# Moving steps on the time line of a hand-ordered attention and Fourier-mixing kernel

## The chip, the core and the metric

The kernel runs on one core of one Trainium2 chip. A core has five engines that each work through their own list of instructions in order: TensorE (PE in the profile: matmuls and transposes, with PEld for its weight loads), VectorE (DVE), ScalarE (ACT), GpSimd (POOL) and SyncE (SP), which here only issues DMA transfers. An instruction that needs what another engine makes waits for a semaphore, and everything behind it on its engine waits with it. The metric is the device time of one execution in microseconds (us), the median of several runs.

## The reference

Two parts follow each other. The first is an attention without a square score matrix, the second mixes tokens and columns with a Fourier transform and ends in a two-layer network:

```python
# q, k, v: (8 batches, 8 heads, 576 tokens, 64)
q_s = softmax(q, axis=-1)
k_s = softmax(k, axis=tokens)
kv  = einsum('bhsd,bhse->bhde', k_s, v)
att = einsum('bhsd,bhde->bhse', q_s, kv)
x   = att as (8, 576, 512)

u   = x + real(fft(fft(x, axis=1), axis=2))
un  = (u - mean(u)) / sqrt(var(u) + 1e-6)        # over the 512 columns
out = u + relu(un @ w_ch1) @ w_ch2               # 512 -> 2048 -> 512
```

All of it is float32.

## The kernel before

**Tiles.** A batch's 576 tokens are 512 in four tiles of 128, and 64 left over. The left-over tokens of two batches share a tile ("shared tokens"); the eight such halves make a ninth group of 512 tokens. So the network runs over nine groups of 512 tokens in the order 0 to 6, the shared group, 7. Group 0 is worked as plain matmuls while the weights arrive. The eight that follow are called stages 1 to 8 here. Stage n works the network of its group, and beside it the attention, Fourier mixing and normalization of the next one (in the code b = order + 1), so stage 2 prepares batch 3, stage 3 batch 4, and so on. Stage 7 has only the norm of the last group beside it, stage 8 nothing.

**A stage.** The two layers are an *up* half (`up`) and a *down* half (`down`). Both use Strassen's scheme in Winograd's form: seven products of quarter matrices in the order 1, 6, 5, 7, 2, 4, 3 in place of eight, with sums before and after. Their products collect in three PSUM banks: products 1 and 2 in `ba`, 6, 7 and 4 in `bb`, 5 and 3 in `bc`. Product 7 adds onto what 6 left in its bank, so an engine has to have read the sum of 6 (u2 = bb + s1, L1137 in the up half, L1290 in the down half) before 7 may begin, and the same holds for 4 after 7 (u3). The final sums of the up half are L1178 on DVE, and ACT's ReLU (L1179, L1174) follows; POOL forms the input sums of the next layer (`a_side`, L389 to L392). The down half of stages 2 to 7 (`deep_down`) applies the scheme twice: one plain product (`single`, L1262), then six of the inner problems in three units of two, each with seven products (L1283). Before a unit its inputs need four sums per product (`a_step`, L1238), three on DVE and one on POOL. After a unit POOL adds results into x (`into`, L1242). Stage 1 cuts the second layer's weights for this on the way (`deepen`, L1202) and writes them to device memory (L1208, w2d), from where later stages read them (L447).

**Work beside the products.** For each next batch: four key blocks (`k_load` L577 to L591, `k_exp` L618 to L630, `k_turn`, `k_times_v`), four query tiles (`q_load` L694, `q_exp` L719 to L738, `q_turn`, `q_times_kv`), and for even batches the shared tokens' tile (`t_load`, `t_turn` L766, `t_fold` L778 to L787, then `t_times_kv` L823 to L838). Then `folded` adds and subtracts mirrored tokens and columns (L854, L860, L869, L875, L876), `block` multiplies by the token table (L910, L913), `mix_own` and `mix_shared` by the column table (L947, L950, with the copy L956, the sums L968/L969 and the additions into x L980/L981). Last comes `norm`: statistics (L1001, L1002), root (L1005), scales (L1008, L1009), a dummy exponential that brings ACT's exponential table back (L1016), normalized tile (L1030), transposes on PE (L1036), their copies (L1044), and four sums for Strassen's scheme (`combine`, L396 to L399), which the next stage's up half reads.

**What sets the order.** From stage 1 on there is no scheduler: `timed` gives every step a number, its time on a script, all steps are sorted by it, and each engine gets its instructions in that order. A number is a place in a list, not a time of the hardware: an instruction runs when its engine reaches it and its data is there. An up half is 56 units long (`UP`), a deep down half 50 (`TWICE`), and two units hold one up product. The steps' own lists (`return [(0, top), (0.8, exp), (4.5, inverse)]`) are relative, and `at(t, ...)` moves them. The attention of the next batch has a `start` and an `end` of 45 within the stage: 0 in stage 1, -7 (in the stage ahead) in the later ones. All loads and most stores are issued from the SP list, so a load can also stand behind a store that waits. A stored tile whose tokens run backwards goes through device memory: written to a `mirror` tensor (L1418), then read back reversed (L1420), which must wait until the first transfer has landed.

Of the kernel before, what the change touches and what calls it, by code (L numbers as in the profile page):

```python
# [93 lines left out]
def at(t, script):  # L94
    return [(t + dt, step) for dt, step in script]
# [42 lines left out]
class _Block:  # L138
# [356 lines left out]
    def attention_timed(self, b, start, end):  # L495

        keys = [("k", b, r) for r in range(NR)]
        tail = [("t", b)] if b % 2 == 0 else []
        own = [("q", b, c, u) for c in range(2) for u in range(2)]
        first = start + 14 + 5 * len(tail)  # L500
        gap, steps = (end - 13 - first) / 3, []
        for i, it in enumerate(keys):
            t = start + 3.5 * i
            steps += at(t - 5.5, self.k_load(it)) + at(t, self.k_exp(it)) + at(t + 4, self.k_turn(it))
            steps += at(t + 7, self.k_times_v(it))
        for it in tail:
            t = start + 14
            steps += at(t - 6.5, self.t_load(it)) + at(t, self.q_exp(it)) + at(t + 8, self.t_turn(it))
            steps += at(t + 10, self.t_fold(it))
        for i, it in enumerate(own):  # L510
            t = first + gap * i
            steps += at(t - 6.5, self.q_load(it)) + at(t, self.q_exp(it)) + at(t + 8, self.q_turn(it))
            steps += at(t + 11, self.q_times_kv(it))
        return steps + at(start + 14 + (23 if tail else 15), self.t_times_kv(b))

    def second_keys(self):

# [326 lines left out]
    def folded(self, b):  # L844


        nc, V, G = self.nc, self.nc.vector, self.nc.gpsimd
        eo = self.eo.setdefault(b, {})

        def tokens_folded(some):  # L850
            for i in some:
                e, op = ((V if b == 0 else G), ALU.add) if i < 2 else (V, ALU.subtract)
                eo[i] = self.halves()
                e.tensor_tensor(out=eo[i][:, 0:D], in0=self.xpart(b, i % 2, 0), in1=self.xpart(b, i % 2, 1), op=op)  # L854

        def columns_folded(some):
            for i in some:
                e, op = ((V if b == 0 else G), ALU.add) if i < 2 else (V, ALU.subtract)
                t = eo[i]
                e.tensor_tensor(out=t[:, 1:HD], in0=t[:, 1:HD], in1=t[:, D - 1:HD:-1], op=op)  # L860
                if b == 0 and i > 1:
                    self.warm(t[:, 0:HD], 2)

        def by_frequency(some):

            for i in some:
                e, op = ((G, ALU.add), (G, ALU.subtract), (V, ALU.add), (V, ALU.subtract))[i]
                one, two = eo[i // 2 * 2], eo[i // 2 * 2 + 1]
                (V if b == 0 else e).tensor_tensor(out=eo[i][:, NN:], in0=one[:, 0:NN], in1=two[:, 0:NN], op=op)  # L869

        def columns_again(some):

            for i in some:
                t, y = eo[i], eo[i][:, NN:]
                V.tensor_tensor(out=t[:, 0:QD], in0=y[:, 0:QD], in1=y[:, HD:QD:-1], op=ALU.subtract)  # L875
                V.tensor_tensor(out=y[:, 0:QD], in0=y[:, 0:QD], in1=y[:, HD:QD:-1], op=ALU.add)  # L876

        def fetch():
            if b == 0:
                self.folded_at = eo[1][:, NN:]  # L880
            elif b + 1 < B:
                self.keys_from(b + 1, eo[1])

        steps = []
        for some, times in ((2, 3), (1, 4.5, 6, 8)), ((0, 1), (0, 4, 6, 12)):
            for f, t in zip((tokens_folded, columns_folded, by_frequency, columns_again), times):
                steps.append((t, lambda f=f, some=some: f(some)))
        return steps + [(12.2, fetch)]
# [103 lines left out]
    def norm(self, g):  # L992
# [4 lines left out]
        uns, box = {}, {}  # L997
# [67 lines left out]
            put(9, scales, s)  # L1065
            put(9.1, back)
        for n, i in enumerate((0, 2, 1, 3)):
            put(10 + 2 * n, normal, i)
            put(12 + 2 * n, turn, i)
            put(12.8 + 2 * n, laid, i)  # L1070
        put(20, combine)
        return steps

    def norm_steps(self, g):
# [139 lines left out]
    def deep_down(self, g, order):  # L1214
# [100 lines left out]
        for i, unit in enumerate(UNITS):  # L1315
            t = 8 + n * i
            for k, o in enumerate((4, 5, 2, 6)):
                for j, m in enumerate(unit):
                    put((0 if i == 0 else t - n + 2) + 3 * k + j * 1.2 + 0.3, a_step, m, o)
            for k, o in enumerate(ORDER):  # L1320
                for j in range(2):
                    put(t + 2 * k + j, product, unit, o, j)
                put(t + 2 * k + 1.5, ends, unit, o)
        t = 8 + n
        put(t + 1, into, 1, 0, 4)
        put(t + 3, into, 0, 0, 2)
        t += n
        put(t + 1, sums, 6, 1)
        put(t + 3, into, 0, 1, 6)
# [69 lines left out]
    def store(self, g, c, u, x, d=None):  # L1399
# [17 lines left out]
            box.append(t[:, s])  # L1417
            e.dma_start(box[0], x())  # L1418

        return [(0, there), (5, lambda: e.dma_start(cols(out)[:, ::-1, :], cols(box[0])))]  # L1420


@with_exitstack
def kernel(ctx: ExitStack, tc: tile.TileContext, q, kT, v, w1, w2, ft,
# [24 lines left out]
    def timed(t, order, g):  # L1449
# [2 lines left out]
        if order == B:  # L1452
            return steps + [(t + 6 + 1.2 * i, lambda i=i: blk.later and blk.later.pop(0)()) for i in range(36)]
        if b == B:
            return steps + at(t + UP + 24, blk.norm(groups[b]))
        start, end = -7 if order > 1 else 0, 45
        steps += at(t, blk.attention_timed(b, start, end)) + at(t + end, blk.folded(b))
        t += UP
        for i, k in enumerate((2, 3, 0, 1, 4)):
# [2 lines left out]
        if b % 2:  # L1462
            mixes.insert(0 if b == B - 1 else 2, blk.mix_shared(b // 2))
        for i, some in enumerate(mixes):
            steps += at(t + 13 + 4 * i, some)
        return steps + at(t + 24, blk.norm(groups[b]))

    fetch, convert = blk.weights()

# [127 lines left out]
```

## Time and profile before

The time before is 1136.15 us, the median of three runs (1134.88 to 1137.81). The profiled execution spans 1130.9 us.

| half | from, us | length, us |
|---|---|---|
| stage 1 up, down | 194.5, 256.9 | 62.4, 59.1 |
| stage 2 up, down | 316.0, 387.9 | 72.0, 57.5 |
| stage 3 up, down | 445.4, 512.1 | 66.7, 56.1 |
| stage 4 up, down | 568.2, 631.0 | 62.8, 57.5 |
| stage 5 up, down | 688.5, 756.7 | 68.2, 56.1 |
| stage 6 up, down | 812.8, 875.6 | 62.8, 57.6 |
| stage 7 up, down | 933.2, 981.6 | 48.4, 47.4 |
| stage 8 up, down | 1029.0, 1077.4 | 48.4, 50.0 |

A half is counted from its first product (L1167 for up; L1361, L1262 or L1283 for down) to the first of the next. In the profile, matmuls are pipelined and each fp32 matmul leaves two records, so a busy share says less than the distance between the starts of neighbours: a longer distance than usual is a hole. A line of the timeline has start and length in us, the engine, the line of the code, the operation, written tile <- read tiles, shapes, the count where equal instructions are merged, and in brackets how long the engine sat idle and what ended that.

### The profile page before, as it was taken

To read this page: it belongs to the slowest core of one execution; us is meant where nothing else is said; L and a number is where in the kernel's file an instruction comes from. 1 tells how busy PE (TensorE), PEld (TensorE's weight loads), DVE (VectorE), ACT (ScalarE), POOL (GpSimd) and SP (SyncE) were. 2 spreads that over 40 slices of the span, in tenths; PEclk is the share of its full clock that TensorE was granted. 3 is DMA by queue.
4 is the path that set the end of the run, shared out by engine and by line. 5 is a ranking of instruction groups with operands and counts; after the bars stand their busy time and mean duration, and the time that the engine had idled before them with its cause. 6 is when DMAs were issued, how large, how long until landed. Compare 5 with 4: busy or idle time off the path is not lost.

```text
span 1130.9 us, 16763 instructions
## 1 busy us (share of the span) xinstructions
PE 1067.4 (94%) x6240; PEld 919.1 (81%) x6240; DVE 657.6 (58%) x1295; ACT 413.5 (37%) x997; POOL 468.6 (41%) x399
## 2 busy tenths in 40 slices
PE   5799999999979999999999999999999999999998
PEld 4644456988868899788998899789998988899887
DVE  6784795665635775666655675667556662473201
ACT  6595424542225214442344233522453132222200
POOL 1064671255403535254433632464516443454420
PEclk9999999999989999999999999999999999999999
DMA  9566676438974566536673566546664566485451
GB/s 310 169 221 196 244 272 220 156 149 269 352 248 149 193 206 218 198 140 231 227 274 139 187 213 234 174 170 227 222 210 147 194 202 224 171 279 194 179 186 56
DMA packets 114480, 233.25 MB, mean 206 GB/s; under 512 B 24272, under 2 KB 76240, under 8 KB 104160
## 3 DMA queue, kind: packets, MB, share of 16 engines
q1 hardware_dynamic: 112600, 231.15, 60.0%
q10 hardware_dynamic: 1800, 1.05, 0.3%
q8 instruction: 49, 0.80, 0.3%
q14 instruction: 31, 0.25, 0.1%
HBM read 197.04 MB, written 39.32 MB: 209 GB/s over the span
## 4 chain that ended last, share of the span: by engine, by line
PE 72%; DVE 11%; issue 2%; DMA 2%; POOL 1%; ACT 1%; SPq 1%; DVEq 0%; POOLq 0%; ACTq 0%
PE bb L1167 13%; PE ba L1167 8%; PE bc L1167 8%; PE bb L1283 7%; PE bc L1283 5%; PE ba L1283 4%; PE bb L1262 3%; PE bb L1361 3%; PE acc L799 2%; PE acc L667 2%; PE ba L1361 2%; PE bc L1361 2%; PE bc L1112 2%; DVE big L1238 2%; DMA q<-in_q_dram 2%
## 5 line engine op out<-in xcount | busy, mean ns | idle before, releaser
L1167 PE MATMUL bb<-unT,big 128*128 128x256 f32 x768 | 185.5, 381 | 4.7 <-DVE u L1137 4.1
L389 POOL TENSOR_TENSOR big<-big 128x512 f32<-128x512 f32 (+1 forms) x38 | 46.7, 1229 | 296.0 <-ACT big L1179 295.2
L1167 PEld LDWEIGHTS bb<-unT,big 128*128 128x128 f32 x768 | 142.7, 191 | 24.6 <-DVE u L1137 4.9
L1179 ACT ACTIVATE big<-big 128x512 f32<-128x512 f32 x96 | 60.2, 629 | 196.3 <-DVE big L1178 196.2
L1167 PE MATMUL ba<-unT,big 128*128 128x256 f32 x512 | 125.6, 383 | 0.2 <-ACT unT L1044 0.2
L1167 PE MATMUL bc<-unT,big 128*128 128x256 f32 x512 | 124.4, 379 | 0.0
L1137 DVE TENSOR_TENSOR u<-bb,s 128x512 f32<-128x512 f32 x68 | 47.0, 691 | 123.1 <-PE bb L1167 85.2
L1167 PEld LDWEIGHTS ba<-unT,big 128*128 128x128 f32 x512 | 96.2, 193 | 13.0 <-ACT unT L1044 0.5
L1283 PE MATMUL bb<-big 128*128 128x128 f32 x768 | 96.7, 276 | 10.7 <-DVE u L1290 10.7
L1167 PEld LDWEIGHTS bc<-unT,big 128*128 128x128 f32 x512 | 94.4, 190 | 12.2 <-DVE big L1178 0.9
L1283 PEld LDWEIGHTS bb<-big 128*128 128x128 f32 x768 | 90.5, 192 | 12.8 <-DVE u L1290 12.8
L1242 POOL TENSOR_TENSOR x<-x,big 128x512 f32<-128x512 f32 x45 | 63.2, 1412 | 65.2 <-issue 27.6
L725 ACT ACTIVATE q<-q,qm 128x64 f32<-128x64 f32 x240 | 63.9, 338 | 30.4 <-DVE qm L719 25.9
L1283 PE MATMUL ba<-big 128*128 128x128 f32 x576 | 72.0, 275 | 0.0
L1283 PEld LDWEIGHTS ba<-big 128*128 128x128 f32 x576 | 68.9, 192 | 1.2
L1238 DVE TENSOR_TENSOR big<-big 128x512 f32<-128x512 f32 x84 | 63.2, 784 | 2.5 <-POOL big L392 2.5
L1290 DVE TENSOR_TENSOR u<-bb,s 128x256 f32<-128x256 f32 x36 | 14.9, 415 | 78.1 <-PE bb L1283 78.1
L1178 DVE TENSOR_TENSOR big<-bc,u 128x512 f32<-128x512 f32 x64 | 44.0, 688 | 25.9 <-PE bc L1167 24.9
L1262 PE MATMUL bb<-big 128*128 128x256 f32 x192 | 44.6, 382 | 9.0 <-DVE big L1178 9.0
L1238 POOL TENSOR_TENSOR big<-big 128x512 f32<-128x512 f32 x24 | 32.5, 1362 | 45.2 <-DVE big L1238 43.3
L1262 PEld LDWEIGHTS bb<-big 128*128 128x128 f32 x192 | 36.0, 190 | 16.3 <-DVE big L1178 11.0
L390 POOL TENSOR_TENSOR big<-big 128x512 f32<-128x512 f32 (+1 forms) x38 | 47.7, 1256 | 2.5
(276 smaller groups left out, 2113.7 us busy)
## 6 DMA issues: line engine op xcount, KB each, us to landing
big<-w2d SPq DMA_DIRECT2D x60, 1024.0 KB
big<-w1s SPq DMA_DIRECT2D x64, 896.0 KB
big<-w2s SPq DMA_DIRECT2D x20, 1024.0 KB
big<-in_w_dram SPq DMA_DIRECT2D x21, 512.0 KB
w2d<-big SPq DMA_DIRECT2D x42, 256.0 KB
q<-in_q_dram SPq DMA_DIRECT2D x27, 256.0 KB
k<-in_kT_dram SPq DMA_DIRECT2D x24, 288.0 KB
v<-in_v_dram SPq DMA_DIRECT2D x24, 256.0 KB
```

Of the source, the lines that this page charges most:

```text
L389: e1.tensor_tensor(out=to(4), in0=at(2), in1=at(3), op=ALU.add)
L390: e1.tensor_tensor(out=to(2), in0=at(0), in1=at(2), op=ALU.subtract)
L725: nc.scalar.activation(q[:, h, :], q[:, h, :], ACT.Exp, bias=m[:, h:h + 1])
L1137: plus = lambda t: V.tensor_tensor(out=temp(t), in0=box["bb"][:], in1=box["s1"][:], op=ALU.add)
L1167: nc.tensor.matmul(bank()[:, i, :], lhsT=w[:, WA_AT[m], k * P:(k + 1) * P], rhs=self.unT[g][:, B_AT[m], k, :], start=first and i == 0 and ...
L1178: steps = [(0, lambda: V.tensor_tensor(out=hp(i), in0=bank()[:], in1=u()[:], op=ALU.add)), (0.8, lambda: nc.scalar.activation(hp(i), hp(i) ...
L1179: (0.8, lambda: nc.scalar.activation(hp(i), hp(i), ACT.Relu))]
L1238: e.tensor_tensor(out=to(o), in0=to(x), in1=to(y), op=op)
L1242: G.tensor_tensor(out=x, in0=x, in1=tile(m), op=ALU.add)
L1262: nc.tensor.matmul(box["bb"][:, i, :], lhsT=h[p][:, A_AT[1], i * P:(i + 1) * P], rhs=self.stream[base][:, p, :], start=i == 0 and p == 0, ...
L1283: nc.tensor.matmul(box[place[n]][:, i, :], lhsT=own(m)(A_AT[n])[:, f, :], rhs=w[:, r // 2, r % 2 * P:r % 2 * P + P], start=first and f == ...
L1361: nc.tensor.matmul(bank()[:, i, :], lhsT=h[p][:, A_AT[m], i * P:(i + 1) * P], rhs=w[:, p, :], start=first and i == 0 and p == 0, stop=p == ...
```

## The change

Numbers on the script are changed and nothing else; every instruction stays. Its parts:

- `timed`: stage 2's attention starts at 0 instead of -7, so that its key loads come after stage 1's writes of cut weights.
- `attention_timed`: the shared tokens' folds go from 17 to 21 in stages 3 and 5 and from 24 to 35 in stage 1, their product from 30 to 33 and from 37 to 42.
- `folded`: the sine side's folds come 0.5 to 1 unit later, the last of them past an addition of the up half.
- `deep_down`: the last unit's input sums come earlier and closer together (from 22.3 on the down half's own count instead of 24.3), and two additions into x go from 23 and 25 to 29 and 31.
- `timed` and `norm`: the mixes come closer together and the norm starts 5 units later, with its tiles 1.3 units apart instead of 2.
- `store`: the mirrored read-back follows the write by 9 units instead of 5.

```diff
@@ attention_timed
-            steps += at(t + 10, self.t_fold(it))
+            steps += at(21 if start < 0 else 35, self.t_fold(it))
...
-        return steps + at(start + 14 + (23 if tail else 15), self.t_times_kv(b))
+        return steps + at((33 if start < 0 else 42) if tail else 22, self.t_times_kv(b))
@@ folded
-        for some, times in ((2, 3), (1, 4.5, 6, 8)), ((0, 1), (0, 4, 6, 12)):
+        for some, times in ((2, 3), (1, 5, 6.5, 9)), ((0, 1), (0, 4, 6, 12)):
@@ norm
         for n, i in enumerate((0, 2, 1, 3)):
-            put(10 + 2 * n, normal, i)
-            put(12 + 2 * n, turn, i)
-            put(12.8 + 2 * n, laid, i)
-        put(20, combine)
+            put(9.3 + 1.3 * n, normal, i)
+            put(10.8 + 1.3 * n, turn, i)
+            put(11.6 + 1.3 * n, laid, i)
+        put(16.5, combine)
@@ deep_down
-                    put((0 if i == 0 else t - n + 2) + 3 * k + j * 1.2 + 0.3, a_step, m, o)
+                    early = 0 if i == 0 else t - n + 2 if i == 1 else t - n
+                    put(early + (3 if i < 2 else 2) * k + j * 1.1 + 0.3, a_step, m, o)
...
-        put(t + 1, into, 1, 0, 4)
-        put(t + 3, into, 0, 0, 2)
+        put(t + 7, into, 1, 0, 4)
+        put(t + 9, into, 0, 0, 2)
@@ store
-        return [(0, there), (5, lambda: e.dma_start(cols(out)[:, ::-1, :], cols(box[0])))]
+        return [(0, there), (9, lambda: e.dma_start(cols(out)[:, ::-1, :], cols(box[0])))]
@@ timed
-            return steps + at(t + UP + 24, blk.norm(groups[b]))
-        start, end = -7 if order > 1 else 0, 45
+            return steps + at(t + UP + 29, blk.norm(groups[b]))
+        start, end = -7 if order > 2 else 0, 45
...
-            steps += at(t + 13 + 4 * i, some)
-        return steps + at(t + 24, blk.norm(groups[b]))
+            steps += at(t + 12.5 + 3.2 * i, some)
+        return steps + at(t + 29, blk.norm(groups[b]))
```

## The prediction

> **What bounds the kernel now.** I read the page first, for the engine that is never free:
>
> ```profile
> PE 1067.4 (94%) x6240; PEld 919.1 (81%) x6240; DVE 657.6 (58%) x1295; ACT 413.5 (37%) x997; POOL 468.6 (41%) x399
> ```
>
> TensorE (PE) is the bound. Its eight-record products tick evenly when nothing holds them: 1.73 us at L1167, L1262 and L1361 (two script units, so a unit is about 0.87 us), 0.90 us at L1283. So only its holes can be won. I took the holes from the start times of neighbouring matmuls: after 194 us they add up to some 47 us, of which 39 us in holes over 0.25 us. The view of waits, for the weight loads from 190 us on, names what ended them:
>
> ```profile
> PEld bb L1283 <- DVE u L1290: 12.8, 11, 2.0
> PEld bb L1262 <- DVE big L1178: 11.0, 5, 2.2
> PEld acc L667 <- ACT ks L646: 6.9, 2, 5.9
> PEld bb L1167 <- DVE u L1137: 4.9, 2, 2.5
> PEld tr L1036 <- ACT eo L1030: 1.5, 1, 1.5
> ```
>
> Columns: total us, times, longest. Each row is one place of the script. Row 2, in the timeline where stage 2's up half ends:
>
> ```profile
> 385.30 0.70 DVE L875 TENSOR_TENSOR eo<-eo 128x128 f32<-128x128 f32 x1
> 386.04 0.70 DVE L876 TENSOR_TENSOR eo<-eo 128x128 f32<-128x128 f32 x1
> 386.66 0.28 DVE L875 TENSOR_TENSOR eo<-eo 128x128 f32<-128x128 f32 x1
> 386.98 0.29 DVE L876 TENSOR_TENSOR eo<-eo 128x128 f32<-128x128 f32 x1
> 387.19 0.68 DVE L1178 TENSOR_TENSOR big<-bb,s 128x512 f32<-128x512 f32 x1
> 387.92 1.35 PE L1262 MATMUL bb<-big 128*128 128x256 f32 x5 [1.81 <-DVE big L1178]
> ```
>
> Four folds (columns_again) stand in VectorE's (DVE's) queue ahead of the addition that reads bank bb; the next product writes bb and waits. Row 3 is one hole in stage 2:
>
> ```profile
> 324.02 0.59 SPq L577 DMA_DIRECT2D k<-in_kT_dram  x1
> ...
> 330.37 0.75 DVE L618 TENSOR_REDUCE km<-k 128x1 f32<-128x576 f32 x1 [7.37 <-DMA k<-in_kT_dram]
> ...
> 332.68 0.58 PE L667 MATMUL acc<-v,ks 128*128 128x128 f32 x1 [5.46 <-ACT ks L646]
> ```
>
> The keys were asked for at 324.02, behind stage 1's stores, and landed over 6 us later; DVE, then ScalarE (ACT), then PE waited. Row 1, in the second of the three units of stage 2's down half:
>
> ```profile
> 421.54 0.39 DVE L1290 TENSOR_TENSOR u<-bb,s 128x256 f32<-128x256 f32 x1
> ...
> 421.99 2.05 PE L1283 MATMUL bb<-big 128*128 128x128 f32 x16 [0.78 <-DVE u L1290]
> ...
> 423.95 1.27 POOL L1238 TENSOR_TENSOR big<-big 128x512 f32<-128x512 f32 x1 [5.89 <-DVE big L1238]
> ...
> 424.54 1.22 DVE L1238 TENSOR_TENSOR big<-big 128x512 f32<-128x512 f32 x1
> ...
> 427.19 1.28 ACT L1016 ACT_TABLE_LOAD   x1
> ```
>
> Product 7 adds into bb, so the sum of product 6 must be read first; DVE reached it late, after statistics and additions. A DVE sum takes 0.6 alone and 1.22 beside GpSimd (POOL).
>
> **What the Trainium skill says.** "SBUF — State Buffer", section "Who interferes with whom": a DVE instruction with two SBUF inputs contends with a POOL instruction that reads SBUF. The trace agrees: the x additions at L980/L981 take 0.42 us alone and 1.49 beside POOL's L1242 at 415.3. "ScalarE: Activation LUTs", "What ACT_TABLE_LOAD costs": some 1.28 us, and 1.38 for a drain. The trace has the 1.28; the first load (2.67 to 3.95) is followed by its activation at 3.96, so no drain shows. "TensorE: Matmul & The Clock Gate", "What's actually happening": an idle window of about 3.4 us halves the clock. After the 5.5 us wait, ten matmuls of L667 took 2.50 us, 1.11 elsewhere: it agrees.
>
> **The change part by part** (stages as in the text above; "after" orders from the built programs).
>
> *A, keys of stage 2 seven units later.* The late key load now has its place 7 units on, as in stage 1, whose up half (same start of 0) loses 0.8 us in all. Stage 2's up half takes 71.97 us, stage 4's, with the same work, 62.79: 9.2 us, made of holes of 0.76 and 5.63 and 2.8 of slow clock. The key and value loads still stand behind stage 1's stores, in a DMA system that its view shows full until about 330. The third key block's tile comes free at about 320; some 1.7 MB then lie ahead of it, at 340 GB/s 5 us, of which about 2 have passed: landing at 323 to 324, wanted by DVE at 322.4 and by PE (through the bank sum behind it on DVE) at about 325. Kept back: 1.0 (bounds 0 to 4). **-8.2.** The mirrored read-back, 4 units later, stops holding the store queue (4.8 us here); nobody on PE waits for it elsewhere: 0.
>
> *B, folds 0.5 to 1 unit later.* In the built order the four folds (1.9 us) stand behind the L1178 addition, which then starts at 385.30 and ends at 386.0, when PE ends its last up product (385.93). Five boundaries have that hole of 1.97; stages 1 and 7 have none. The folds themselves are wanted by the first block 2 units later: covered by the two products before it. 5 x 1.9, **-9.3** (bounds -7 and -9.8).
>
> *C, last unit's sums, stores into x, and norm.* Holes in the down halves of stages 2 to 6: 2.23, 1.97, 2.23, 1.97, 2.91, together 11.3. In the second unit, ahead of the L1290 that reads product 6, DVE now has no statistics (two x 0.83) and no POOL additions beside it (2.1 us of stretch); three more L1238 sums of the last unit (0.6 each) come in. From the end of the first unit DVE then has 4.8 us of work with three mixes (stages 2, 4, 6), 5.2 with that L1290, against the 5.4 that three products give. Ahead of product 7's L1290, two L1238 beside POOL (1.2 to 1.75 each) and one statistic remain: 0 to 1.2 over in those three stages, I take 0.6; and 0.2 in each of the five for the first unit, where a second L1238 of the next unit now precedes product 6's L1290. 11.3 - 1.8 - 1.0 = **-8.5** (bounds -5 and -11). In stage 7 the same exchange puts one more 0.6 us sum ahead of an L1290 that PE already waits for: **+0.6**.
>
> *D, folds of shared tokens.* Stages 3 and 5 have a hole of 2.21 where L778, L780 and L781 (beside POOL) precede L1137. Now they follow that addition and precede the next, for which PE leaves 2.6 us more. Stage 5 also loses 1.7 to a slower clock (its view shows 0.97). 4.4 + 1.7, kept back 0.5: **-5.6** (bounds -2, -6). Holes of about 0.55 twice in each, behind the q load, stay. In stage 1 the folds get idle DVE time: 0.
>
> *E, norm of stage 1.* Its first transpose waits 1.26; five units later it finds its data: **-1.2**.
>
> *N, what the change adds.* In the after order of ACT, stages 2 to 7, the copy of product 1 of the last unit (L1297) now stands between the root (L1005) and the table load of L1016. Before, that load ran early (427.19 above, with DVE's scales still to come). Now it can begin only when PE has ended product 1: 0.24 to the copy's start (433.09 after 432.85), 0.37 copy, 1.28 load, 0.20 L1016, 0.81 L1030, 0.08 hand-overs: 2.98 us to the first normalized tile. PE has product 6 to do, 1.79. It waits 1.19, six times: **+7.1**. Behind the waiting ACT stand the later tiles (spaced 1.4 us on ACT against 1.57 on PE) and laid-out copies; the transforms for the next stage end about 1.9 us before it: no second wait. Bounds: 0, if the load overlaps the wait, to 2.57 each (the page's drain added), 15.4.
>
> Sum: -8.2 - 9.3 - 8.5 + 0.6 - 5.6 - 1.2 + 7.1 = -25.1; 1136.15 - 25.1 = **1111**.
>
> **The rivals.** (1) The table load is hidden or hurts little and C is free: -25.1 - 7.1 - 2.8 - 1.5 (what A and D kept back) gives about 1100. For it: loads have run ahead of waits in this trace. Against: they stand behind an in-order copy that itself waits. (2) DVE is only re-queued: C gives 3 instead of 8.5, the early sums collide with POOL, keys still come 4 us late, the drain shows in half of the six: +5.5 + 3 + 4, about 1123. For it: DVE works 38.9 of 57.5 us in such a half, and each removed hole brings PE nearer to it. (3) Slower: the late norm ends after PE. If transposes, copies and POOL's 1.77 us transform each ended 5 us late in the seven stages, +35 - 25 gives 1146. For it: its steps come 1.3 units apart instead of 2. Against: I count 1.9 us of room at a stage's end, and PE does 8 us of products beside them.
>
> **How the numbers follow.** Forecast 0.60, rival 1 0.15, rival 2 0.17, rival 3 0.08. The time is the forecast's. The range from 1100 to 1125 takes in the forecast's bounds and the first two rivals' middles; what it leaves out is the third and the tails. Faster: 0.60 + 0.15 + 0.16 = 0.91; same 0.02; slower 0.07.
>
> **What would show it.** Right: L1262 no longer waits for L1178; L667's 5.5 us hole and the 0.95 clock of stage 2 are gone; L1036 waits for ACT L1030 six times by about 1.2, with each table load directly behind L1297. Wrong: L1036 without waits (then about 1104), L1290 waits as long as before, L1167 of a next stage waiting for the transforms (L396 to L399), or L618 still waiting for keys with PE behind it.

## The result, and the profile after

The changed kernel takes 1119.59 us (median of four runs, 1118.32 to 1121.62); the kernel before takes 1136.98 beside it. The ratio is 0.9851, with a 95% interval of 0.9828 to 0.9874: 1.5%, or 17 us, less, where 25 us were forecast. The profiled execution spans 1119.8 us, 11.1 less than that of before. This pair shows less than the medians do, because the profiled execution of before lies below its kernel's other runs (1132.71 us) and that of the changed kernel is the longest of its four (1121.62). Of the experiments below, the profiled execution of the one with early scales was disturbed (1818.72 us), and its times are not used. In the changed kernel, lines from 1319 on have moved by one: L1361, L1378, L1418 and L1420 are now L1362, L1379, L1419 and L1421.

The page's first part, for the kernel after, has the same number of instructions on every engine:

```profile
PE 1065.1 (95%) x6240; PEld 917.4 (82%) x6240; DVE 651.6 (58%) x1295; ACT 412.1 (37%) x997; POOL 484.4 (43%) x399
```

POOL is busy for 16 us more (468.6 before), and the other engines for a little less. Only holes could go, and the lengths of the halves show where they went:

| half | before, us | after, us | difference |
|---|---|---|---|
| stage 1 up, down | 62.39, 59.10 | 64.46, 59.00 | +2.07, -0.10 |
| stage 2 up, down | 71.97, 57.50 | 67.45, 57.31 | -4.52, -0.19 |
| stage 3 up, down | 66.67, 56.12 | 63.92, 55.09 | -2.75, -1.03 |
| stage 4 up, down | 62.79, 57.50 | 60.83, 57.01 | -1.96, -0.49 |
| stage 5 up, down | 68.18, 56.12 | 62.56, 55.10 | -5.62, -1.02 |
| stage 6 up, down | 62.80, 57.63 | 60.82, 57.14 | -1.98, -0.49 |
| stage 7 up, down | 48.35, 47.45 | 48.35, 49.21 | 0, +1.76 |
| stage 8 up, down | 48.35, 50.00 | 48.35, 50.00 | 0, 0 |

The halves sum to -16.3. The first product starts 1.3 later (195.8 for 194.5; over all traces of the study that are read this start lies between 193.3 and 196.5, so it is no effect of the change), and the stretch from the last product to the end of the span grows from 3.5 to 7.4. -16.3 + 1.3 + 3.9 = -11.1.

The view of waits of the kernel after, for the weight loads from 190 us on (total us, times, longest); the views below leave out lines of instructions that the reading does not need:

```profile
PEld tr L1036 <- ACT eo L1030: 9.1, 7, 1.9
PEld bb L1167 <- DVE krec L629: 7.0, 3, 3.7
PEld bb L1283 <- DVE u L1290: 4.4, 7, 1.8
PEld tr L746 <- DVE q L738: 3.3, 4, 1.2
PEld bb L1167 <- DVE u L1137: 2.2, 1, 2.2
PEld bb L1262 <- DVE big L1178: 1.0, 5, 0.2
```

Row 6 was 11.0 with 2.2 as its longest: the folds' holes are gone. Row 3 was 12.8. Row 1 was 1.5, once: it is the wait that the prediction said the change would add. Rows 2 and 5 are the surprises: the keys still come late, now seen from another matmul, and a hole has opened in stage 1. Row 4 was 2.0, three times: a hole of 0.98 ahead of L746 in stage 2 is new.

**Row 6**, in the timeline of the kernel after where stage 2's up half ends:

```profile
384.75 1.28 DVE L869 TENSOR_TENSOR eo<-eo 128x257 f32<-128x257 f32 x2
385.95 0.68 DVE L1178 TENSOR_TENSOR big<-bb,s 128x512 f32<-128x512 f32 x1
386.55 0.28 DVE L875 TENSOR_TENSOR eo<-eo 128x128 f32<-128x128 f32 x1
386.71 1.10 PE L1262 MATMUL bb<-big 128*128 128x256 f32 x4
```

The addition L1178 now stands ahead of the folds L875, and L1262 starts with no bracket behind it: PE waited for nothing, and the 0.2 us of row 6 are a wait of its weight load. The hole of 1.97 is gone at all five boundaries.

**Row 1**, in the timeline of the kernel after, last unit of stage 2's down half:

```profile
430.09 0.37 ACT L1297 COPY s<-ba 128x256 f32<-128x256 f32 x1 [2.35 <-PE ba L1283]
430.48 1.28 ACT L1016 ACT_TABLE_LOAD   x1
...
431.89 1.50 ACT L1030 ACTIVATE eo<-x,mv,std 128x512 f32<-128x512 f32 x2
432.74 0.66 PE L1036 MATMUL tr<-ident,eo 128*128 128x128 f32 x4 [1.25 <-ACT eo L1030]
```

ACT sat idle for 2.35 us at the copy, with the table load behind it, and the load then ran while PE had nothing left: the distances between matmuls give holes of 1.41, 1.12, 1.12, 1.11, 1.11 and 1.12 in stages 2 to 7, 7.0 together.

**Row 2**, the keys of stage 2 in the timeline of the kernel after:

```profile
323.74 3.94 SPq L1419 DMA_DIRECT2D mirror<-x  x1
...
327.80 0.36 SPq L577 DMA_DIRECT2D k<-in_kT_dram  x1
...
332.07 0.75 DVE L618 TENSOR_REDUCE km<-k 128x1 f32<-128x576 f32 x1 [7.15 <-DMA k<-in_kT_dram]
332.86 0.69 DVE L1137 TENSOR_TENSOR u<-bb,s 128x512 f32<-128x512 f32 x1
...
333.60 2.08 PE L1167 MATMUL bb<-unT,big 128*128 128x256 f32 x4 [3.33 <-DVE krec L629]
```

SP's own list held the third key block: the issue of one mirrored store took 3.94 us where the others of its kind take 0.3 to 1.1, and the key load stood behind it. It was asked for at 327.80, which is 8.5 us into the stage (it begins at 319.26), and DVE had it at 332.07. In the kernel before, it was the fourth key block that came late, asked for 8.1 us into the stage (324.02) and on DVE at 330.37. PE waits in L1167 now, since DVE's addition of the bank, L1137, stands behind the keys.

**Row 5**, stage 1 in the timeline of the kernel after:

```profile
251.37 1.23 DVE L838 TENSOR_TENSOR eo<-eo 128x128 f32<-128x128 f32 x1
252.53 0.68 DVE L1137 TENSOR_TENSOR u<-bb,s 128x512 f32<-128x512 f32 x1
253.26 1.99 PE L1167 MATMUL bb<-unT,big 128*128 128x256 f32 x8 [1.83 <-DVE u L1137]
```

Here the shared tokens' product, moved from 37 to 42, brings its own folds (L835 to L838) ahead of the addition L1137 that PE needs. A 128x128 fold takes 1.23 beside POOL; L875, of the same shape, takes 0.28 in the fence of row 6.

**Not in a row of its own:** in stage 3 a hole behind the late query rows grew from 0.55 to 2.09 (0.38 to 0.73 in stage 5). The same two places held 0.4 to 1.3 us in the four profiled executions with the order of before, and up to 2.1 or nothing clear in six with the order of the change, so it is not shown that the change made it grow. In the timeline of the kernel after, DVE waits for the transfer, and L1137 behind it for DVE:

```profile
458.27 0.69 DVE L719 TENSOR_REDUCE qm<-q 128x8 f32<-128x512 f32 x1 [5.26 <-DMA q<-in_q_dram]
458.99 0.69 DVE L1137 TENSOR_TENSOR u<-bb,s 128x512 f32<-128x512 f32 x1
459.74 1.13 PE L1167 MATMUL bb<-unT,big 128*128 128x256 f32 x4 [1.92 <-DVE krec L629]
```

The waits view puts this hole, too, down to L629, which had long been done; the line that had just ended on DVE is L1137. And at the end, the timeline of SP and ACT in the kernel after:

```profile
1108.77 0.32 SPq L1419 DMA_DIRECT2D mirror<-x  x1
1112.35 1.85 SPq L1421 DMA_DIRECT2D out_dram<-mirror  x2
1113.02 0.34 ACTq L1412 DMA_DIRECT2D out_dram<-x  x1
```

Both of SP's mirrored read-backs (L1421) are now issued after the last mirrored write, together. In the kernel before, one went out at 1120.73, ahead of the last write at 1123.76, the other at 1125.45, before the last product's end at 1127.38.

### The profile page after: what moved, and what is told of

It reads as the page before. It is cut to its first block, busy times and chain, and to the rows that moved or that the text cites. A ratio compares the mean times of both kernels' runs of the same rounds, so it can differ in the third digit from the quotient of the medians.

```text
span 1119.8 us, 16766 instructions
## 1 busy us (share of the span) xinstructions
PE 1065.1 (95%) x6240; PEld 917.4 (82%) x6240; DVE 651.6 (58%) x1295; ACT 412.1 (37%) x997; POOL 484.4 (43%) x399
## 4 chain that ended last, share of the span: by engine, by line
PE 74%; DVE 8%; issue 2%; DMA 2%; POOL 2%; ACT 2%; SPq 1%; POOLq 0%; DVEq 0%; ACTq 0%
PE bb L1167 14%; PE ba L1167 9%; PE bc L1167 9%; PE bb L1283 7%; PE bc L1283 5%; PE ba L1283 5%; PE bb L1262 3%; PE bb L1362 3%; PE acc L667 2%; PE acc L799 2%; DVE big L1238 2%; PE bc L1362 2%; PE ba L1362 2%; PE bc L1112 2%; PE acc L910 2%
## 5 line engine op out<-in xcount | busy, mean ns | idle before, releaser
L1167 PE MATMUL bb<-unT,big 128*128 128x256 f32 x768 | 185.3, 381 | 7.7 <-DVE krec L629 5.8
L1167 PEld LDWEIGHTS bb<-unT,big 128*128 128x128 f32 x768 | 143.0, 191 | 27.8 <-DVE krec L629 7.0
L1167 PE MATMUL ba<-unT,big 128*128 128x256 f32 x512 | 124.1, 379 | 0.2 <-ACT unT L1044 0.2
L1167 PE MATMUL bc<-unT,big 128*128 128x256 f32 x512 | 124.1, 379 | 0.0
L1137 DVE TENSOR_TENSOR u<-bb,s 128x512 f32<-128x512 f32 x68 | 46.9, 690 | 127.8 <-PE bb L1167 88.6
L1167 PEld LDWEIGHTS ba<-unT,big 128*128 128x128 f32 x512 | 94.6, 190 | 12.3 <-ACT unT L1044 0.5
L1167 PEld LDWEIGHTS bc<-unT,big 128*128 128x128 f32 x512 | 94.5, 190 | 12.1 <-DVE big L1178 0.5
L1283 PEld LDWEIGHTS bb<-big 128*128 128x128 f32 x768 | 90.3, 192 | 4.4 <-DVE u L1290 4.4
L1242 POOL TENSOR_TENSOR x<-x,big 128x512 f32<-128x512 f32 x45 | 71.9, 1608 | 32.7 <-DVE big L1290 16.1
L725 ACT ACTIVATE q<-q,qm 128x64 f32<-128x64 f32 x240 | 64.3, 338 | 41.0 <-DVE qm L719 30.1
L1238 DVE TENSOR_TENSOR big<-big 128x512 f32<-128x512 f32 x84 | 74.9, 934 | 2.5 <-POOL big L392 2.5
L1238 POOL TENSOR_TENSOR big<-big 128x512 f32<-128x512 f32 x24 | 37.1, 1556 | 60.7 <-DVE big L1238 60.7
L1178 DVE TENSOR_TENSOR big<-bc,u 128x512 f32<-128x512 f32 x64 | 44.0, 687 | 24.0 <-PE bc L1167 23.1
L1290 DVE TENSOR_TENSOR u<-bb,s 128x256 f32<-128x256 f32 x36 | 15.0, 418 | 67.6 <-PE bb L1283 67.3
L1283 PE MATMUL bc<-big 128*128 128x128 f32 x384 | 46.8, 275 | 0.0
L624 ACT ACTIVATE k<-k,km 128x576 f32<-128x576 f32 x24 | 18.6, 776 | 76.4 <-DVE km L618 51.9
```

Source lines behind the costliest of these rows:

```text
L725: nc.scalar.activation(q[:, h, :], q[:, h, :], ACT.Exp, bias=m[:, h:h + 1])
L1137: plus = lambda t: V.tensor_tensor(out=temp(t), in0=box["bb"][:], in1=box["s1"][:], op=ALU.add)
L1167: nc.tensor.matmul(bank()[:, i, :], lhsT=w[:, WA_AT[m], k * P:(k + 1) * P], rhs=self.unT[g][:, B_AT[m], k, :], start=first and i == 0 and ...
L1178: steps = [(0, lambda: V.tensor_tensor(out=hp(i), in0=bank()[:], in1=u()[:], op=ALU.add)), (0.8, lambda: nc.scalar.activation(hp(i), hp(i) ...
L1238: e.tensor_tensor(out=to(o), in0=to(x), in1=to(y), op=op)
L1242: G.tensor_tensor(out=x, in0=x, in1=tile(m), op=ALU.add)
```

## The experiments

Times are medians; ratios are to the kernel before, run on the same chip, with 95% intervals. The experiments differ from the kernel that they start from, the minus side of each diff, in script numbers alone.

**The added wait (N).** The changed kernel, with the scales early enough that the table load stands ahead of the copy.

```diff
-            put(9, scales, s)
-            put(9.1, back)
+            put(8, scales, s)
+            put(8.2, back)
```

> The changed kernel, but scales and the dummy exponential of the norm stand one unit earlier (8 and 8.2 instead of 9 and 9.1), so that the table load of L1016 precedes the copy L1297 on ACT. Theory (step N): the six holes of 1.1 to 1.4 us ahead of the transposes L1036 in the deep halves come from the table load that waits behind that copy; they vanish, 7 us less than the changed kernel, about 1112.6. Rival: the tiles are late for another reason (statistics or scales late on DVE); the holes stay within 0.3 us of what they are and the time stays at 1119 to 1120.

1111.47 us (median of three), ratio 0.976 (0.9727 to 0.9792): 8 to 10 us less than the changed kernel, a little more than the 7.0 of the six holes. In its trace, of which only the order is used, the load stands ahead of the copy L1297 in stages 2 to 7; the times that go with this order are seen below, in the version with five repairs. The load's place, not its 1.28 us, costs the time.

**One part alone: the folds (B).** The kernel before, with the fold times of the change.

```diff
-        for some, times in ((2, 3), (1, 4.5, 6, 8)), ((0, 1), (0, 4, 6, 12)):
+        for some, times in ((2, 3), (1, 5, 6.5, 9)), ((0, 1), (0, 4, 6, 12)):
```

> The kernel before with the fold times of the change alone. Theory (step B): the five holes of 1.97 us ahead of L1262 close and nothing opens: 9.3 to 9.9 less than before, about 1127.3. Rival: PE comes earlier to sums that DVE has not made yet and the holes come back at L1283 or at the first blocks L910: less than 5 us gained, 1132 or more.

1123.84 us, ratio 0.9881 (0.9855 to 0.9907); its profiled span is 1121.6, 9.3 less than that of before. The five holes of 1.97 are gone and none opened. By the holes more than half of the gain, by the medians 13 of 17 us, is in three numbers.

**One part alone: the early sums and the later additions into x (half of C).** The kernel before, with the edits of `deep_down`.

```diff
-                    put((0 if i == 0 else t - n + 2) + 3 * k + j * 1.2 + 0.3, a_step, m, o)
+                    early = 0 if i == 0 else t - n + 2 if i == 1 else t - n
+                    put(early + (3 if i < 2 else 2) * k + j * 1.1 + 0.3, a_step, m, o)
...
-        put(t + 1, into, 1, 0, 4)
-        put(t + 3, into, 0, 0, 2)
+        put(t + 7, into, 1, 0, 4)
+        put(t + 9, into, 0, 0, 2)
```

> The kernel before with the edits of the deep down half alone (input sums of the last unit earlier, two additions into x later). Theory: three more sums (1.8 us) come into the same stretch of DVE from which POOL's collisions (2.1 us) go, with the statistics still there: holes ahead of the second unit's L1290 about as before, time within 3 us of before. Rival (the collisions alone made the holes): the down halves of stages 2 to 6 lose their 11.3 us of holes, 1127 or less.

1152.0 us, ratio 1.0117 (1.0081 to 1.0152): 15 us slower, a clear miss. The timeline of this experiment, second unit of stage 2's down half:

```profile
423.17 1.73 DVE L1238 TENSOR_TENSOR big<-big 128x512 f32<-128x512 f32 x1
424.82 0.41 DVE L1290 TENSOR_TENSOR u<-bb,s 128x256 f32<-128x256 f32 x1
425.29 2.05 PE L1283 MATMUL bb<-big 128*128 128x128 f32 x16 [1.51 <-DVE u L1290]
...
429.12 0.68 DVE L1001 BATCH_NORM_STATS2 st<-x 128x6 f32<-128x512 f32 x1
...
430.73 0.39 DVE L1290 TENSOR_TENSOR u<-bb,s 128x256 f32<-128x256 f32 x1
431.17 2.82 PE L1283 MATMUL bb<-big 128*128 128x128 f32 x16 [2.04 <-DVE u L1290]
```

A sum stretched beside POOL stands ahead of the first L1290, and the statistics, two of which the prediction saw leave, are still ahead of the second: the two holes grow from 0.94 and 1.29 to 1.67 and 2.21. And the sixteen matmuls after the second hole take 2.82 where those after the first take 2.05: matmuls that start 0.11 apart elsewhere start 0.21 apart from 432.4 to 435.7. The half takes 60.78 for 57.50: 1.65 more of holes and about 1.6 of slow clock (the granted clock is 0.50 from 432.3 to 435.7), in each of stages 2, 4 and 6. Stages 3 and 5 take 0.85 more each, stage 7 2.3.

**One part alone: the mixes closer, the norm later (the other half of C, with N and E).** The kernel before, with the edits of `norm` and of the norm's and mixes' times in `timed` (the last two parts of the change's diff, without the line of `start`).

```diff
-            put(10 + 2 * n, normal, i)
+            put(9.3 + 1.3 * n, normal, i)
...
-            steps += at(t + 13 + 4 * i, some)
-        return steps + at(t + 24, blk.norm(groups[b]))
+            steps += at(t + 12.5 + 3.2 * i, some)
+        return steps + at(t + 29, blk.norm(groups[b]))
```

> The kernel before with the moves of the mixes and of the norm alone. Theory: without statistics in the second unit most of the 11.3 us of holes there go (8 to 10), and the table load behind L1297 brings six holes of about 1.1 to 1.2 (7 us): 1 to 3 us less than before, 1134 to 1136. Rival (the norm's later place costs nothing): 8 us or more less than before, 1129 or less, no waits at L1036.

1130.78 us, ratio 0.9955 (0.9936 to 0.9975): 6 us less than before, and 3 to 5 less than expected. The timeline of this experiment, at the same place:

```profile
422.14 0.41 DVE L1290 TENSOR_TENSOR u<-bb,s 128x256 f32<-128x256 f32 x1
...
422.86 1.95 PE L1283 MATMUL bb<-big 128*128 128x128 f32 x16
...
425.09 0.39 DVE L1290 TENSOR_TENSOR u<-bb,s 128x256 f32<-128x256 f32 x1
...
426.43 1.95 PE L1283 MATMUL bb<-big 128*128 128x128 f32 x16
```

Both L1290 are early and PE waits for neither. The down halves of stages 2 to 6 take 5.9 us less than before although each has the new hole of 1.12; without it that is 11.5. So the new places of norm and mixes alone win all that C could win, and the early sums have no part in it. Where the kernel before has four statistics (L1001) ahead of these two L1290, from 418.60 on, one is left here, at 424.27; what the mixes add to this was not run apart. In the changed kernel the early sums are a cost: the page's group of L1238 on DVE, first of this experiment, then of the kernel after, with the mean in ns behind the busy time:

```profile
L1238 DVE TENSOR_TENSOR big<-big 128x512 f32<-128x512 f32 x84 | 60.2, 761 | 2.5 <-POOL big L392 2.5
```

```profile
L1238 DVE TENSOR_TENSOR big<-big 128x512 f32<-128x512 f32 x84 | 74.9, 934 | 2.5 <-POOL big L392 2.5
```

The same 84 sums take 14.7 us longer in the changed kernel, which has them earlier and closer together, beside POOL's. In the last two versions below, with the early sums and without, they take 73.3 and 64.3, so not all of the 14.7 is theirs.

**The keys' move undone (A).** The changed kernel, with stage 2's attention at -7 again.

```diff
-        start, end = -7 if order > 2 else 0, 45
+        start, end = -7 if order > 1 else 0, 45
```

> The changed kernel with stage 2's attention back at -7. Theory (step A as put on record): moving it by seven units was worth 8.2 us, so undoing it costs that, about 1128. Rival (the keys are still late because the transfers queued by stage 1 are done no earlier than 330): most of the gain was lost to a new wait for the same transfers, and undoing it costs 2 to 4 us, 1122 to 1124.

1118.16 us, ratio 0.9848 (0.9806 to 0.9891): no different from the changed kernel. Stage 2's up half takes 67.84 for 67.45. No worth of the keys' move shows. It has a cost, too: the new hole of 0.98 ahead of L746 in stage 2 is gone here. It is there in all eight traces with the move that are read, and in none of the five without it.

**The transfers ahead of the keys.** The changed kernel, with stage 1's stores, and the read-backs behind them, 16 units later.

```diff
-        nc, own = self.nc, g < B
+        nc, own, late = self.nc, g < B, 16 if g == 1 else 0
...
-            return [(0, lambda: e.dma_start(out, x()))]
+            return [(late, lambda: e.dma_start(out, x()))]
...
-        return [(0, there), (9, lambda: e.dma_start(cols(out)[:, ::-1, :], cols(box[0])))]
+        return [(late, there), (late + 9, lambda: e.dma_start(cols(out)[:, ::-1, :], cols(box[0])))]
```

> The changed kernel with the four stores of stage 1's output (and their read-backs) 16 units later, behind stage 2's key and value loads. Theory (transfers queued ahead of the key load make it late): the third key block is asked for some 4 to 6 us earlier, the hole of 3.5 us in stage 2's up half and its slow clock shrink: 3 to 5 us less than the changed kernel, 1115 to 1117. Rival (the stores don't matter, the cut weights alone fill the transfer engines until then): the hole stays within 1 us, 1119 to 1120.

1113.61 us, ratio 0.9795 (0.9758 to 0.9833). Its timeline, at the same key block:

```profile
323.69 0.33 SPq L577 DMA_DIRECT2D k<-in_kT_dram  x1
...
326.79 0.75 DVE L618 TENSOR_REDUCE km<-k 128x1 f32<-128x576 f32 x1 [2.55 <-DMA k<-in_kT_dram]
...
327.57 0.69 DVE L1137 TENSOR_TENSOR u<-bb,s 128x512 f32<-128x512 f32 x1
...
332.57 0.43 SPq L1419 DMA_DIRECT2D mirror<-x  x1
```

The third block is asked for at 323.69, 5.1 us into the stage instead of 8.5, with the mirrored store behind it, and DVE has it 3.1 us later instead of 4.3. PE's hole and the slow clock after it are gone: the half takes 62.28, 5.2 less than in the changed kernel, and the two versions at the end, with the same edit, take 62.29. The cause of row 2 is the stores ahead of the load: between these two executions, they cost 3.4 us on SP's list and 1.2 in the transfers.

**Stage 1 as before (D's and E's part there).** The changed kernel, with the times of the kernel before for stage 1's shared tokens, and its norm at 26.4.

```diff
-            steps += at(21 if start < 0 else 35, self.t_fold(it))
+            steps += at(21 if start < 0 else 24 if b == 2 else 35, self.t_fold(it))
...
-        return steps + at((33 if start < 0 else 42) if tail else 22, self.t_times_kv(b))
+        return steps + at((33 if start < 0 else 37) if tail else 22, self.t_times_kv(b))
...
-        return steps + at(t + 29, blk.norm(groups[b]))
+        return steps + at(t + (29 if order > 1 else 26.4), blk.norm(groups[b]))
```

> The changed kernel with stage 1 alone mended: the shared tokens' folds and product back at 24 and 37, and its norm starting at 26.4 instead of 29. Theory: the hole of 1.99 us at L1167 (three folds of L835 to L838 beside POOL, ahead of the bank sum) and that of 1.71 at stage 1's first transpose go: 3.3 to 3.9 less than the changed kernel, about 1116. Rival: stage 1 is held by its transfers, and what PE gains there it loses at the keys of stage 2: within 1.5 us of the changed kernel.

1114.83 us, ratio 0.9806 (0.9777 to 0.9835). Stage 1's up half is back at 62.39 (for 64.46): the hole of 1.99 came with the move of the folds and their product, and it is the product's own lines that stand ahead of L1137 in the fence of row 5. The transpose's hole went from 1.71 to the 1.26 of the kernel before and no further, so a later start of the norm does not close it, as the prediction's E had it. The down half takes 58.55. These two halves explain 2.5 of the 4.8 us between the medians; stage 3's hole of 2.09 happened to be smaller here as well (its half takes 62.39 for 63.92), and why is not known.

**The shared query rows asked for earlier.** The changed kernel, with that load 8 units earlier in stages 3 and 5.

```diff
-            steps += at(t - 6.5, self.t_load(it)) + at(t, self.q_exp(it)) + at(t + 8, self.t_turn(it))
+            steps += at(t - (14.5 if start < 0 else 6.5), self.t_load(it)) + at(t, self.q_exp(it)) + at(t + 8, self.t_turn(it))
```

> The changed kernel with the load of the shared tokens' rows 8 units earlier in stages 3 and 5. Theory: the holes of 2.09 and 0.73 us there (DVE waits for these rows ahead of a bank sum) and the two of 0.54 behind it shrink: 2 to 4 us less than the changed kernel, 1116 to 1118. Rival: the rows' own wait (the last of the five transfers is issued only when the other four have landed) now holds the key loads behind it, and the same time comes back at L667: 1119 or more.

1118.85 us, ratio 0.9837 (0.979 to 0.9883): no clear difference from the changed kernel. The trace is clearer: the holes of 2.09 and 0.73 are gone (the halves take 61.73 and 62.02 for 63.92 and 62.56), while stage 2's key hole was larger in this execution (4.6 for 3.5).

**The read-back at 5 again.** The changed kernel, with the mirrored read-back as before.

```diff
-        return [(0, there), (9, lambda: e.dma_start(cols(out)[:, ::-1, :], cols(box[0])))]
+        return [(0, there), (5, lambda: e.dma_start(cols(out)[:, ::-1, :], cols(box[0])))]
```

> The changed kernel with the mirrored read-back at 5 units instead of 9. Theory (costed at 0): within 1.5 us of the changed kernel, 1118 to 1121. Rival: at 5 it blocks the list of loads again, the keys of stage 2 and the shared rows come later: 2 to 5 us more.

1121.83 us, ratio 0.9858 (0.9829 to 0.9887): 2 us more, inside the scatter. But two opposite effects hide in it. Stage 2's up half takes 72.82 for 67.45, with a key hole of 7.85; the end after the last product takes 3.6 for 7.4. SP issues nothing from 315.2 to 319.25, where the read-back waits for its write; four writes of cut weights then go out ahead of the keys, and the third block, asked for 7.6 us into the stage, needs 9.6 us to land. The longest wait for keys in stage 2 (the longest in the rows of L667 or L629, one profiled execution each) gathers the runs that leave stage 1's stores in their place:

| | read-back at 5 | read-back at 9 |
|---|---|---|
| keys at -7 | 5.9, 6.1, 5.8, 5.7 | 4.1 |
| keys at 0 | 8.1 | 3.7, 4.4, 4.9, 5.9 |

The later read-back, costed at 0 in the prediction, shortens the wait in both lines; the keys' move doesn't in either column, though two of the four fields hold one execution each. The column on the right also shows how much one and the same place differs from execution to execution.

**The end.** The changed kernel, with the read-back at 5 for the last group of tokens alone.

```diff
-        return [(0, there), (9, lambda: e.dma_start(cols(out)[:, ::-1, :], cols(box[0])))]
+        return [(0, there), (5 if g == B - 1 else 9, lambda: e.dma_start(cols(out)[:, ::-1, :], cols(box[0])))]
```

> The changed kernel, with the read-back of the mirrored stores at 5 units again for the last group of tokens alone, 9 for all others. Theory: the 3.9 us by which the end behind the last product grew (3.5 to 7.4 us) come from the last group's read-backs, of which two are now issued together after the last mirrored write, at 1112.35 us; spread again as before, the stretch after the last product goes back to about 3.5 us and the time to about 1116 us (1119.6 less 3 to 4), with every product stage unchanged. Rival: the end is set by the last transfers whatever their order, or a stage in front gives the time back: within 1.5 us of 1119.6.

1117.86 us, ratio 0.9836 (0.9811 to 0.9861): 1.7 less than the changed kernel, with overlapping ranges. In its timeline SP sends one read-back before the last write and one after it:

```profile
1107.56 0.69 SPq L1421 DMA_DIRECT2D out_dram<-mirror  x1
...
1110.58 0.32 SPq L1419 DMA_DIRECT2D mirror<-x  x1
...
1113.70 0.67 SPq L1421 DMA_DIRECT2D out_dram<-mirror  x1
```

The end takes 4.8 for 7.4. But in both executions the last write landed late: the read-back behind it went out 3.1 us after it here and 3.6 in the changed kernel, where the kernel before has 1.7. Of the executions with 1.7, five with the order of before (the kernel before, the folds alone, the norm alone, the read-back at 5, the last version below) end 3.3 to 3.6 us after the last product, and four with the order of the change (the keys' move undone, stage 1 as before, the early query rows, the five repairs) 5.2 to 5.5. So some 1.9 of the 3.9 are the order. The other 2.0 are the late landing, which is no effect of the change: the run with the early sums alone, with the order of before, has it too and ends after 5.2. The profiled spans, 1119.0 and 1119.8, hardly differ because the wait for the keys was 5.9 in this execution.

**Five repairs together.** The changed kernel with the early scales, the late stores, stage 1 as before, the early query rows, and 1.2 in place of 1.1 between the sums of the first two units (this puts stage 7's order back).

```diff
-                    put(early + (3 if i < 2 else 2) * k + j * 1.1 + 0.3, a_step, m, o)
+                    put(early + (3 if i < 2 else 2) * k + j * (1.2 if i < 2 else 1.1) + 0.3, a_step, m, o)
```

> The changed kernel with the four mends together: the norm's dummy exponential earlier, stage 1's stores later, stage 1's folds and norm back, the shared rows' load earlier, and the two sums of stage 7 behind the bank sum again. If the costs add up as located: 7 + 4 + 3.7 + 3 + 0.6, some 18 us less than the changed kernel, about 1101. Rival (waits pass from one to the next): less than half of it, 1110 or more.

1099.78 us, ratio 0.9666 (0.9638 to 0.9694): the costs add up as they were found one by one. By the traces they are 7.0 for the six holes, 5.2, 2.5 and 2.7 for the halves that the next three repairs change, and 0.6 for stage 7, 18.0 together; the halves are 18.6 shorter than in the changed kernel. Its timeline, at the place of row 1:

```profile
417.93 1.28 ACT L1016 ACT_TABLE_LOAD   x1
...
419.97 0.37 ACT L1297 COPY s<-ba 128x256 f32<-128x256 f32 x1 [0.54 <-PE ba L1283]
...
420.24 1.52 ACT L1030 ACTIVATE eo<-x,mv,std 128x512 f32<-128x512 f32 x2
...
421.50 0.60 PE L1036 MATMUL tr<-ident,eo 128*128 128x128 f32 x4
```

The load runs ahead of the copy, in time in which ACT had nothing else, and L1036 waits for nothing.

**And the early sums taken out.** The version with five repairs, with the edits of `deep_down` undone and the last group's read-back at 5.

```diff
-                    early = 0 if i == 0 else t - n + 2 if i == 1 else t - n
-                    put(early + (3 if i < 2 else 2) * k + j * (1.2 if i < 2 else 1.1) + 0.3, a_step, m, o)
+                    put((0 if i == 0 else t - n + 2) + 3 * k + j * 1.2 + 0.3, a_step, m, o)
...
-        put(t + 7, into, 1, 0, 4)
-        put(t + 9, into, 0, 0, 2)
+        put(t + 1, into, 1, 0, 4)
+        put(t + 3, into, 0, 0, 2)
```

> The version with five repairs (1099.8 us), and in it the early sums of the last unit and the two moves of the additions into the factor undone (as in the kernel before), with the last group's read-back at 5. Theory: with the statistics moved away, the early sums only cost: the holes at the second unit (about .47 in stages 2, 4 and 6, .8 in stage 6) and the .6 us of stage 7 go, about 2.5 us, and the end gives about 2 us: near 1095 us. Rival: the sums are needed and their return reopens the holes of 1 to 2 us at the second unit, as in the run with the sums alone: 1099 us or more.

1096.7 us (1095.16 to 1098.57), ratio 0.9651 (0.9624 to 0.9677): the fastest version of the study, 3.1 us under the last by the medians and 1.7 by the ratios, whose intervals overlap. The traces show the places. Its rows of waits that belong here:

```profile
PEld bb L1283 <- DVE u L1290: 1.6, 2, 1.2
PEld tr L1036 <- ACT eo L1030: 1.5, 1, 1.5
```

The second-unit holes of stages 2, 4 and 6 are gone, but for 0.4 in stage 6 (their down halves take 55.04, 55.04 and 55.01 for 55.84, 55.84 and 55.97, 2.6 less), and the end takes 3.3 for 5.2. The early sums cost, once the statistics stand elsewhere.

## Why the prediction was right in direction and 8 us too far

Each step of the sum, against what the profiled pair shows for the same place:

| step | forecast | measured | from |
|---|---|---|---|
| A, keys | -8.2 | -2.5 | stage 2 up -4.5, less B's 1.97 |
| B, folds | -9.3 | -9.9 | five holes of 1.97 |
| C, down halves 2 to 6 | -8.5 | -9.1 | halves -3.2, less N's 5.9 there |
| C, stage 7 | +0.6 | +0.6 | +1.76, less N's 1.12 |
| D, stages 3 and 5 | -5.6 | -4.4 | halves -8.4, less B's 3.9 |
| D, stage 1 | 0 | +2.1 | the half |
| E, stage 1's norm | -1.2 | -0.1 | the half |
| N, table load | +7.1 | +7.0 | six holes |
| read-back at the end | 0 | +3.9 | 3.5 to 7.4, some 1.9 of it by the change |
| start | - | +1.3 | not of the change |
| sum | -25.1 | -11.1 | |

**B, N and stage 7 were right, and tested.** B needed only the built order and the durations of four folds. N is the step that held best: one table load, put behind a copy that waits for PE, was worked out at 1.19 us per stage and measured at 1.11 to 1.41. Rival 1, which hid it, is out; so is the part of rival 2 in which a drain shows in half of the six. The experiment that moves the load ahead gave the time back.

**C had the right size and half a wrong reason.** The prediction said DVE gains because the statistics leave and because POOL's additions leave its side. The move of norm and mixes did it alone (-11.5 in those halves without the sums' edits); the early sums took about 2.4 of this back, with L1238 stretched beside POOL, and on their own made the kernel 15 us slower. The sum came out near -8.5 because the residues assumed (0.6 and 0.2 a stage, 2.8 in all) happened to be near this cost: the size was in part luck.

**A failed.** "Landing at 323 to 324" was the step. On the clock of the kernel before, that is 7 to 8 us into stage 2; 12.8 was measured (332.07, in a stage that begins at 319.26). It took the bytes ahead divided by a rate as the time of the load, and left out what happens on SP's list: one store's issue took 3.94 us, and the load wasn't asked for until 8.5 us into the stage. It also laid stage 2's excess on the keys' place, while putting the mirrored read-back at 0. The runs show the contrary: undoing the keys' move leaves the time as it is, the read-back's four units shorten the wait, and taking stage 1's stores away from the front of the loads wins 5.2 us in that half. Rival 2 had this part right ("keys still come 4 us late"). The -2.5 is the difference of two executions, and the same wait differs by up to 2.2 us between executions of one order.

**The read-back at the end failed as a zero.** "Nobody on PE waits for it" is true and was not enough: behind the last product nothing hides a transfer, and the order of the last stores is the end of the program. Some 1.9 of the 3.9 us are shown to be this; the rest is a late landing that other orders show too.

**D and E failed in stage 1.** "The folds get idle DVE time: 0" looked at the shared folds, not at the product that moves with them and brings L835 to L838, 1.2 to 1.4 us each beside POOL, ahead of L1137: +2.1. E took the norm's start for the cause of a hole that stays at 1.26 when the norm starts 2.6 units earlier, and grows to 1.71 with the change. In stages 3 and 5, the holes of 0.55 "behind the q load" did not simply stay: one was 2.09 in this execution, and it varies as much from one execution to the next.

The steps' errors sum to 5.7 + 2.1 + 1.2 + 1.1 + 3.9 - 0.6 - 0.6 - 0.1 = 12.7, and with the start's 1.3 to the 14 by which the profiled pair falls short. Against the medians the shortfall is 8. How the other 6 divide among steps is open: they are differences between executions, of which the wait for the keys, 3.7 to 5.9 us in four runs with the same order up to there, is one, and the late landing at the end, 2.0 us, another.

## What to carry to other kernels

On engines that work through their lists in order, price an edit by what comes to stand *ahead of* each instruction that the bound engine waits for, and look for the one that itself waits: an early table load costs nothing, the same load behind a waiting copy costs PE 1.1 us each time. A place on the script is not a time for a DMA: ask what stands ahead on the queue that issues it, and move the stores, not the load. And take a bundle of edits apart: here three numbers gave more than half of the gain, one part was a loss inside a winning change, and what single runs showed took the gain from 17 to 39 us.

## What the runs showed of the hardware that was not expected

- An issue on SP is not always short, and what stands just ahead of it matters. In the kernel after, the only issues over 3 us behind 320 us (3.94 at 323.74, then 3.53, 5.20, 4.95 and 5.12 in stages 3 to 6) each stand directly behind a mirrored read-back and begin within 2.3 us of it; issues that came 4 us or more behind one took 0.3. With stage 1's stores later, the long issue moved with its read-back (6.19 at 337.37). What in the read-back holds SP is not shown.
- A hole of 2.2 us can cost clock. In the run with the early sums alone, matmuls started 0.21 apart, for 0.11, from 432.4 to 435.7, behind holes of 1.67 and 2.21. In the kernel before, a hole of 2.21 in stage 5 was followed by a granted clock of 0.50 from 716.9 to 720.3, and the hole of 2.21 in stage 3 by none below 1.00. What decides is not shown. The Trainium skill ("TensorE: Matmul & The Clock Gate", "What's actually happening") speaks of an idle window of about 3.4 us; none of these holes is that long, and the measurement decides.
- A 128x512 sum on DVE took 1.73 us beside POOL, for 0.6 alone, and POOL's own 24 sums at L1238 went from 1362 to 1556 ns in the mean with the change: the stretch shows on both sides.
